# Row-shaped weight products with 512 moving columns, vectors in blocks of 512 and split row transfers in a one-token decoder block

## The chip, the cores and the metric

The kernel runs on one core of one Trainium2 chip. The metric is the device time of one execution in microseconds (us). The kernel before took 415.2, 415.21 and 415.24 us in three runs, median 415.21. A profiled execution is a further run, with its own time.

## The reference

One token (a row of 1024 numbers, bfloat16) passes a decoder block: layer norm, attention over a cache of 65,536 positions with 32 query heads and 4 key/value heads, output projection, residual; then layer norm, a gated feed-forward layer of width 3584, residual.

```
def _A_ref(x, k_cache, v_cache, wq, wo):          # 32 heads of 128, 4 kv heads
    q = (x @ wq).reshape(B, Sq, Hq, Dh).transpose(0, 2, 1, 3)
    ...
    scores = jnp.einsum("bhqd,bhkd->bhqk", q, k) * (Dh ** -0.5)
    p = _softmax(scores, axis=-1)
    o = jnp.einsum("bhqk,bhkd->bhqd", p, v)
    return o.transpose(0, 2, 1, 3).reshape(B, Sq, Hq * Dh) @ wo

def _B_ref(x, w_gate, w_up, w_down):
    return (_gelu(x @ w_gate) * (x @ w_up)) @ w_down

h = x + _A_ref(_layernorm(x), A_k_cache, A_v_cache, A_wq, A_wo)
h2 = h + _B_ref(_layernorm(h), B_w_gate, B_w_up, B_w_down)
```

Every weight and every cache entry is used once, so 173 MB have to come from memory for one row of output.

## The kernel before

All large transfers go through one queue, SyncE's (SP in the profile), in the order of the source, into a pool of four chunks of 4 MB (`chpool`, 32 KB per partition): two for `wq`, then 32 for the caches, two for `wo`, two each for gate, up and down. A chunk is asked for as soon as the chunk four places earlier has been used up. The framework under the kernel gives each engine its instructions in an order of its own that keeps to the dependences; it isn't always that of the source.

A vector of 1024 stands in columns: partition p holds the 8 neighbours 8p to 8p+7 (`x_col`, `h_col`, L152 and L335). The helper `layernorm_cols` (L126 and after) normalises such a vector; its last step, L145, writes bfloat16 columns (`xn_bf`, `hn_bf`).

**Narrow products.** The products with `wq` (L160), gate and up (`ffn_in`, L357) and down (L397) are made with the weights as the stationary operand: 128x128 weights are loaded, and one column of the vector moves through them, which gives 128 outputs, one to a partition. In gate and up the 128 weights of a load lie 28 numbers apart (`f:F:FC`), in down 8 numbers apart (`j:D:DC`), in q they are neighbours. All of them add into one small PSUM tile that is set to zero first: 256 such products for q, 224 each for gate, up and down.

**Wide products.** The output projection (L324) does it the other way round: the vector, padded with zeros to 32 columns (`o2z`), is the stationary operand, and 512 neighbouring weights of each partition move. Four such products stand side by side in the array, at `tile_position` (0, 32q), and add into the row 32q of a PSUM bank; two banks (`at_ps`) hold the two halves of the 1024 outputs, four partial sums each. The result is a row, not a column: L328 and L330 copy the banks to `at_r`, and eight f32 products against a column of ones (L333) add the partial sums and turn them into columns.

Between the parts of the attention nothing is touched by the change: K chunks are transposed by VectorE (L211) and multiplied (L215), the scores are reduced (L225, L226), the softmax is taken on ScalarE (L248), and V chunks are multiplied (L264, L278). Gate's result goes through an approximate gelu on VectorE and ScalarE (L364 to L374) while up's products run; L377 multiplies both into `act_bf`. Down's weights come in pieces of 10, 6, 4, 3, 2, 1, 1 and 1 rows per partition, and the last of them in three transfers, for 8, 8 and 112 partitions. L402 adds the residual, L403 stores the 2 KB of output.

Of the kernel before, what the change touches and what calls it, by code (L numbers as in the profile page):

```python
# [17 lines left out]
def kernel(  # L18
# [13 lines left out]
    nc = tc.nc  # L32
# [18 lines left out]
    DCH = 2  # L51
    CW = DCH * CH * Dh
    assert NCH % DCH == 0
    scale = float(Dh) ** -0.5
    eps = 1e-5
    assert Dh == P and rep * NS == SQ and NT % (CH * NH) == 0 and D % P == 0 and F % P == 0

    const = ctx.enter_context(tc.tile_pool(name="const", bufs=1))
    small = ctx.enter_context(tc.tile_pool(name="small", bufs=2))
# [16 lines left out]
    wq_v = A_wq.rearrange("(p c) n -> p c n", p=P)  # L76
    WB = CW // HD
    assert WB >= 1 and DC % WB == 0
    XU = 16
    XV = P // XU  # L80
    x_in = const.tile([XU, XV, DC], BF16, name="x_in")
    nc.scalar.dma_start(out=x_in[:], in_=A_x[0, 0].rearrange("(u v c) -> u v c", u=XU, v=XV))
    wq_tiles = []
    for c0 in range(0, DC, WB):
        w_sb = chunk("wq_sb")
        wv = w_sb[:, 0:WB * HD].rearrange("p (c n) -> p c n", c=WB)
        nc.sync.dma_start(out=wv, in_=wq_v[:, c0:c0 + WB, :])  # L87
        wq_tiles.extend(wv[:, i, :] for i in range(WB))


    ones_f = const.tile([P, P], F32, name="ones_f")
# [55 lines left out]

    x_ps = misc([P, DC], F32, "x_ps")
    for v in range(XV):
        nc.tensor.matmul(x_ps[:], lhsT=xsel[:, v, :], rhs=x_in[:, v, :], start=(v == 0), stop=(v == XV - 1))  # L150
    x_col = const.tile([P, DC], F32, name="x_col")
    nc.vector.tensor_copy(out=x_col[:], in_=x_ps[:])  # L152
    xn_bf = const.tile([P, DC], BF16, name="xn_bf")
    layernorm_cols(x_col[:], xn_bf[:], "ln1")

    q_ps = misc([P, Hq], F32, "q_ps")
    nc.vector.memset(q_ps[:], 0.0)
    for c in range(DC):
        for h in range(Hq):
            nc.tensor.matmul(q_ps[:, h:h + 1], lhsT=wq_tiles[c][:, h * P:(h + 1) * P], rhs=xn_bf[:, c:c + 1],  # L160
                             start=False, stop=False, skip_group_check=True)
    qT_bf = const.tile([P, Hq], BF16, name="qT_bf")
    nc.vector.tensor_copy(out=qT_bf[:], in_=q_ps[:])
    qsel_ps = misc([P, 4, Hq], F32, "qsel_ps")
# [149 lines left out]
    NW = D // 512  # L314
    at_ps = [misc([P, 512], F32, "at_ps") for _ in range(NW)]
    for w0 in range(0, Hq, WN):
        w_sb = chunk("wo_sb")
        wv = w_sb[:, 0:WN * D].rearrange("p (c n) -> p c n", c=WN)
        nc.sync.dma_start(out=wv, in_=wo_v[:, w0:w0 + WN, :])
        for cc in range(WN):  # L320
            c = w0 + cc
            q = c % 4
            for s in range(NW):
                nc.tensor.matmul(at_ps[s][32 * q:32 * q + 32, :], lhsT=o2z[:, c, :],  # L324
                                 rhs=wv[:, cc, s * 512:(s + 1) * 512],
                                 start=(c < 4), stop=(c >= Hq - 4), tile_position=(0, 32 * q))
    at_r = ktpool.tile([P, D], F32, name="at_r", tag="kt")
    nc.vector.tensor_copy(out=at_r[:, 0:512], in_=at_ps[0][:])  # L328
    for s in range(1, NW):
        nc.scalar.copy(out=at_r[:, s * 512:(s + 1) * 512], in_=at_ps[s][:])  # L330
    hc_ps = misc([P, DC], F32, "hc_ps")
    for j in range(DC):
        nc.tensor.matmul(hc_ps[:, j:j + 1], lhsT=at_r[:, j:D:DC], rhs=ones_f[:, 0:1], start=True, stop=True)  # L333
    h_col = const.tile([P, DC], F32, name="h_col")
    nc.vector.tensor_tensor(out=h_col[:], in0=hc_ps[:], in1=x_col[:], op=ALU.add)  # L335


    hn_bf = const.tile([P, DC], BF16, name="hn_bf")
    layernorm_cols(h_col[:], hn_bf[:], "ln2")
    GB = max(1, CW // F)  # L340
    assert DC % GB == 0

    def ffn_in(wmat, name, pieces):
        ps = misc([P, FC], F32, name)
        nc.vector.memset(ps[:], 0.0)
        wv_all = wmat.rearrange("(p c) n -> p c n", p=P)
        assert sum(pieces) == DC
        for c0 in range(0, DC, GB):
            w_sb = chunk("wgu_sb")
            wv = w_sb[:, 0:GB * F].rearrange("p (c n) -> p c n", c=GB)  # L350
            r0 = 0
            while r0 < GB:
                sz = pieces.pop(0)
                nc.sync.dma_start(out=wv[:, r0:r0 + sz, :], in_=wv_all[:, c0 + r0:c0 + r0 + sz, :])
                for cc in range(r0, r0 + sz):
                    for f in range(FC):
                        nc.tensor.matmul(ps[:, f:f + 1], lhsT=wv[:, cc, f:F:FC], rhs=hn_bf[:, c0 + cc:c0 + cc + 1],  # L357
                                         start=False, stop=False, skip_group_check=True)
                r0 += sz
        return ps  # L360

    g_ps = ffn_in(B_w_gate, "g_ps", [4, 4])
# [9 lines left out]
    nc.vector.tensor_scalar(out=hg[:], in0=g_sb[:], scalar1=0.5, scalar2=None, op0=ALU.mult)  # L372
    gl = small.tile([P, FC], F32, name="gl", tag="gl")
    nc.vector.scalar_tensor_tensor(out=gl[:], in0=th[:], scalar=1.0, in1=hg[:], op0=ALU.add, op1=ALU.mult)  # L374
    u_ps = ffn_in(B_w_up, "u_ps", [4, 2, 1, 1])
    act_bf = const.tile([P, FC], BF16, name="act_bf")
    nc.vector.tensor_tensor(out=act_bf[:], in0=u_ps[:], in1=gl[:], op=ALU.mult)  # L377


    wd_v = B_w_down.rearrange("(p c) n -> p c n", p=P)  # L380
    DN = CW // D
    pieces = [[10, 6], [4, 3, 2, 1, 1, 1]]
    assert sum(map(sum, pieces)) == FC and max(map(sum, pieces)) <= DN
    d_ps = misc([P, DC], F32, "d_ps")
    nc.vector.memset(d_ps[:], 0.0)
    c0 = 0
    for group in pieces:
        w_sb = chunk("wd_sb")
        r0 = 0
        for sz in group:  # L390
            wv = w_sb[:, r0 * D:(r0 + sz) * D].rearrange("p (c n) -> p c n", c=sz)
            last = c0 + sz == FC
            for lo, hi in ((0, 8), (8, 16), (16, P)) if last else ((0, P),):
                nc.sync.dma_start(out=wv[lo:hi], in_=wd_v[lo:hi, c0:c0 + sz, :])
            for cc in range(sz):
                for j in range(DC):
                    nc.tensor.matmul(d_ps[:, j:j + 1], lhsT=wv[:, cc, j:D:DC], rhs=act_bf[:, c0 + cc:c0 + cc + 1],  # L397
                                     start=False, stop=False, skip_group_check=True)
            c0 += sz
            r0 += sz  # L400
    h2 = small.tile([P, DC], BF16, name="h2", tag="h2")
    nc.vector.tensor_tensor(out=h2[:], in0=d_ps[:], in1=h_col[:], op=ALU.add)  # L402
    nc.sync.dma_start(out=out[0, 0].rearrange("(p c) -> p c", p=P), in_=h2[:])  # L403


# [28 lines left out]
```

## Time and profile before

| what | us |
|---|---|
| median of the runs | 415.21 |
| the profiled execution, its own time | 414.91 |
| its span, first to last instruction | 413.1 |
| first narrow product of gate | 368.13 |
| last narrow product of up ends | 396.66 |
| last narrow product of down ends | 410.50 |
| TensorE busy over the span | 256.8 (62%) |
| VectorE busy over the span | 201.9 (49%) |
| memory read over the span | 419 GB/s |

In the groups of instructions, each row is a line of the code, its engine and operation, output and inputs, shapes and count, then busy time, the mean of one in ns, and the engine's idle time ahead of it with what ended it:

```profile
L357 PE MATMUL g_ps<-hn_bf,wgu_sb 128*128 128x1 bf16 x224 | 14.3, 202 | 1.2 <-DVE hn_bf L145 1.2
L160 PE MATMUL q_ps<-xn_bf,wq_sb 128*128 128x1 bf16 x256 | 7.2, 165 | 10.8 <-DMA wq_sb<-in_A_wq_dram 10.8
L397 PE MATMUL d_ps<-act_bf,wd_sb 128*128 128x1 bf16 x224 | 13.6, 198 | 0.3 <-DVE act_bf L377 0.3
```

The mean of one includes what overlaps the next; busy time over the count is the spacing. PE is TensorE's products, PEld its weight loads, DVE VectorE, ACT ScalarE, POOL GpSimd. The PEclk row of the page is the clock that TensorE was granted, as a share of full speed; it is 0.5 in most of the last 80 us.

### The profile page before, as it was taken

The page shows a single profiled execution, that of the slowest core. Times are in us where ns is not written, and L with a number is a line of the kernel's source. Part 1 is how long each engine was busy: PE and PEld are TensorE (multiplying, and loading weights), DVE is VectorE, ACT ScalarE, POOL GpSimd, SP SyncE. Part 2 cuts the span into 40 slices and gives each one's busy share as a digit, 9 for nine tenths or more (in the row PEclk, how much of TensorE's full clock was granted, in tenths as well). Part 3 has the DMA queues.
Part 4 walks back from the last instruction along what each step waited for, and adds up shares of the span by engine and source line. Part 5 has one row for each costly group of instructions (what it writes and reads, how often), then busy time and mean ns, then how long its engine had stood idle before and what let it go on. Part 6 is the DMA issues. An engine that isn't in the chain of part 4 may idle for free.

```text
span 413.1 us, 4925 instructions
## 1 busy us (share of the span) xinstructions
PE 256.8 (62%) x2117; PEld 138.3 (33%) x2117; DVE 201.9 (49%) x254; ACT 35.9 (9%) x135; POOL 27.1 (7%) x100
## 2 busy tenths in 40 slices
PE   1336677698291838765566388191928335479997
PEld 1332222243130314221222233030314113279997
DVE  3107999999393808856474389291910000010000
ACT  1000000070000080000003400000071000000000
POOL 8123000310000210000000000000000000000000
PEclk9999989989886867895959698777796755655555
DMA  8999999999999999999999999999999999999993
GB/s 356 420 439 432 428 435 424 431 431 427 435 428 435 427 432 428 430 431 431 424 435 428 435 428 433 428 435 427 431 431 427 435 428 436 423 431 414 425 409 115
DMA packets 7413, 173.33 MB, mean 420 GB/s; under 512 B 992, under 2 KB 992, under 8 KB 1888
## 3 DMA queue, kind: packets, MB, share of 16 engines
q1 hardware_dynamic: 7360, 173.02, 98.0%
q8 instruction: 16, 0.26, 0.3%
q14 instruction: 5, 0.04, 0.0%
q10 hardware_dynamic: 32, 0.00, 0.0%
HBM read 173.02 MB, written 0.00 MB: 419 GB/s over the span
## 4 chain that ended last, share of the span: by engine, by line
DMA 52%; DVE 23%; PE 15%; issue 9%; SPq 0%; POOLq 0%; ACT 0%; POOL 0%; ACTq 0%
DMA k_sb<-in_A_k_cache_dram 44%; DVE kt L211 19%; DMA v_sb<-in_A_v_cache_dram 8%; PE g_ps L357 3%; PE u_ps L357 3%; PE d_ps L397 3%; PE qk_ps L215 2%; DVE mx L226 2%; DVE sc L225 2%; PE acc_ps L264 1%; PE o_ps L278 0%; SPq L87 0%; POOLq L429 0%; ACT acc_sb L275 0%; PE mxT_ps L233 0%
## 5 line engine op out<-in xcount | busy, mean ns | idle before, releaser
L215 PE MATMUL qk_ps<-kt,qs 128*128 128x512 bf16 x512 | 143.7, 436 | 78.8 <-DVE kt L211 76.7
L211 DVE STREAM_TRANSPOSE kt<-k_sb 128x1024 f32<-128x1024 f32 x128 | 146.2, 1208 | 53.5 <-DMA k_sb<-in_A_k_cache_dram 53.5
L215 PEld LDWEIGHTS <-qs 128*128 128x128 bf16 x512 | 54.9, 107 | 164.5 <-issue 120.9
L248 ACT ACTIVATE pt<-sc,nbias 128x256 bf16<-128x256 f32 x64 | 31.5, 492 | 275.2 <-DVE nbias L241 275.2
L264 PE MATMUL acc_ps<-v_sb,pt 128*32 128x512 bf16 x512 | 38.0, 444 | 13.5 <-DMA v_sb<-in_A_v_cache_dram 13.5
L357 PEld LDWEIGHTS <-wgu_sb 128*128 128x128 bf16 x448 | 28.5, 172 | 1.3 <-issue 1.3
L280 DVE TENSOR_TENSOR oT_all<-o_ps,rl 128x8 bf16<-128x8 f32 x4 | 0.7, 167 | 55.1 <-PE o_ps L278 55.1
L264 PEld LDWEIGHTS <-pt 128*32 128x32 bf16 x512 | 13.9, 107 | 33.0 <-issue 25.2
L225 DVE STREAM_TRANSPOSE sc<-qk_ps 128x512 f32<-128x512 f32 x32 | 22.1, 692 | 2.1 <-PE qk_ps L215 2.1
L226 DVE TENSOR_REDUCE mx<-sc 128x8 f32<-128x512 f32 x32 | 22.0, 688 | 1.1
L278 PE MATMUL o_ps<-sel,acc_sb 128*128 128x8 f32 x32 | 7.5, 364 | 21.8 <-ACT acc_sb L275 21.8
L357 PE MATMUL g_ps<-hn_bf,wgu_sb 128*128 128x1 bf16 x224 | 14.3, 202 | 1.2 <-DVE hn_bf L145 1.2
L278 PEld LDWEIGHTS o_ps<-sel,acc_sb 128*128 128x128 f32 x32 | 7.1, 328 | 23.0 <-ACT acc_sb L275 23.0
L357 PE MATMUL u_ps<-hn_bf,wgu_sb 128*128 128x1 bf16 x224 | 14.3, 202 | 0.0
L173 POOL MEMSET qs<- 128x2048 bf16 x4 | 7.2, 1803 | 102.6 <-PE qk_ps L215 102.6
L160 PE MATMUL q_ps<-xn_bf,wq_sb 128*128 128x1 bf16 x256 | 7.2, 165 | 10.8 <-DMA wq_sb<-in_A_wq_dram 10.8
L397 PE MATMUL d_ps<-act_bf,wd_sb 128*128 128x1 bf16 x224 | 13.6, 198 | 0.3 <-DVE act_bf L377 0.3
L397 PEld LDWEIGHTS <-wd_sb 128*128 128x128 bf16 x224 | 13.6, 164 | 0.2 <-issue 0.2
L177 POOL COPY qs<-qsel 32x32 bf16<-32x32 bf16 x64 | 11.2, 247 | 17.1 <-DVE qsel L168 16.4
L324 PE MATMUL at_ps<-wo_sb,o2z 128*32 128x512 bf16 x64 | 6.9, 609 | 8.5 <-DMA wo_sb<-in_A_wo_dram 8.5
L248 ACT ACTIVATION_READ_ACCUMULATOR pt<-sc,nbias 128x1 f32 x64 | 11.9, 186 | 0.0
L312 POOL MEMSET o2z<- 128x1024 bf16 x1 | 0.9, 950 | 156.6 <-PE acc_ps L264 156.6
(80 smaller groups left out, 61.3 us busy)
## 6 DMA issues: line engine op xcount, KB each, us to landing
k_sb<-in_A_k_cache_dram SPq DMA_DIRECT2D x16, 4096.0 KB, 29.8
v_sb<-in_A_v_cache_dram SPq DMA_DIRECT2D x16, 4096.0 KB, 33.1
wq_sb<-in_A_wq_dram SPq DMA_DIRECT2D x2, 4096.0 KB, 12.1
wo_sb<-in_A_wo_dram SPq DMA_DIRECT2D x2, 4096.0 KB, 36.5
wgu_sb<-in_B_w_gate_dram SPq DMA_DIRECT2D x2, 3584.0 KB, 33.4
wgu_sb<-in_B_w_up_dram SPq DMA_DIRECT2D x1, 3584.0 KB, 31.6
wd_sb<-in_B_w_down_dram SPq DMA_DIRECT2D x1, 2560.0 KB
wgu_sb<-in_B_w_up_dram SPq DMA_DIRECT2D x1, 1792.0 KB, 26.4
```

The source lines that it names most:

```text
L160: nc.tensor.matmul(q_ps[:, h:h + 1], lhsT=wq_tiles[c][:, h * P:(h + 1) * P], rhs=xn_bf[:, c:c + 1], start=False, stop=False, skip_group_ch ...
L173: nc.gpsimd.memset(qs[:], 0.0)
L177: nc.gpsimd.tensor_copy(out=qs[rows, :, s, SQ * i + s:SQ * (i + 1):NS], in_=qsel[rows, :, g * rep:(g + 1) * rep])
L211: nc.vector.transpose(out=kt[:], in_=k32[:, s * W:(s + 1) * W])
L215: nc.tensor.matmul(qk[:], lhsT=st["qs"][:, jt, s, :], rhs=mv[:, :, J, :, t], start=(s == 0 and jt == 0), stop=(s == NS - 1 and jt == 3))
L225: nc.vector.transpose(out=sc.rearrange("p n h s -> p (n h s)"), in_=qk[:])
L226: nc.vector.tensor_reduce(out=st["mx"][:, :, ci], in_=sc.rearrange("p n h s -> p h n s"), axis=AX.XY, op=ALU.max)
L248: nc.scalar.activation(out=pt[:].rearrange("p c n h s -> p (c n) h s")[:, :, r, :], in_=sc[:].rearrange("p c n h s -> p (c n) h s")[:, :, ...
L264: nc.tensor.matmul(acc[32 * c:32 * c + 32, :], lhsT=pt[:, ci % CPH, n, :, :].rearrange("p h s -> p (h s)"), rhs=v_sb[:, n:CH:NN, :], start ...
L278: nc.tensor.matmul(o_ps[:], lhsT=acc_sb[:, t * Dh:(t + 1) * Dh], rhs=sel[:, t:SQ:NS], start=(t == 0), stop=(t == NS - 1))
L357: nc.tensor.matmul(ps[:, f:f + 1], lhsT=wv[:, cc, f:F:FC], rhs=hn_bf[:, c0 + cc:c0 + cc + 1], start=False, stop=False, skip_group_check=True)
L397: nc.tensor.matmul(d_ps[:, j:j + 1], lhsT=wv[:, cc, j:D:DC], rhs=act_bf[:, c0 + cc:c0 + cc + 1], start=False, stop=False, skip_group_check ...
```

## The change

The change does six things.

1. Vectors stand in blocks of 512: partition p holds the 4 neighbours 4p to 4p+3 of each block (D = 2 blocks, F = 7). The views of all weights, of x and of the output follow; a narrow product's 128 weights now lie 4 numbers apart.
2. q, gate, the first six of up's eight rows per partition and down's first six blocks of seven become wide products. Layer norm writes column 0 of a zeroed tile (`xz`, `actz`) that serves as the stationary operand. In `wide_rows` seven (or eight) blocks of a row go to the four places of two banks.
3. A wide result is copied from its banks (`evacuate`) and turned into columns by f32 products against selection columns: `to_columns` with `sel4` for q, gate and up, eight products each; `fold_columns` with `sel2` for the output projection and down, which use one bank with two partial sums, four products each.
4. Up's last two rows and down's last block stay narrow products. They add into the same PSUM tile as the columns of the wide part.
5. `load_rows` splits a transfer: all rows but the last for 128 partitions, then the last row in three transfers, of n, 16 - n and 112 partitions. It is used for both chunks of `wo` (n = 2, 4) and of gate (6, 3), the first of up (1), and down's first two blocks (5, 7).
6. Down's pieces are blocks of 4 rows; the last block comes as 2, 1 and 1 rows, each for all 128 partitions, and the transfers for 8 and 8 partitions are gone.

```diff
+    def load_rows(dst, src, splits):
+        nr = dst.shape[1]
+        if not splits:
+            nc.sync.dma_start(out=dst, in_=src)
+            return
+        if nr > 1:
+            nc.sync.dma_start(out=dst[:, 0:nr - 1, :], in_=src[:, 0:nr - 1, :])
+        lo = 0
+        for n in list(splits) + [P - sum(splits)]:
+            nc.sync.dma_start(out=dst[lo:lo + n, nr - 1:nr, :], in_=src[lo:lo + n, nr - 1:nr, :])
+            lo += n
...
+    xz = const.tile([P, DC, 32], BF16, name="xz")
+    nc.gpsimd.memset(xz[:], 0.0)
+    layernorm_cols(x_col[:], xz[:, :, 0], "ln1")
+    def wide_rows(banks, rows_z, ci, w_row, first, last):
+        for t in range(w_row.shape[-1] // NB):
+            q = t % 4
+            nc.tensor.matmul(banks[t // 4][32 * q:32 * q + 32, :], lhsT=rows_z[:, ci, :],
+                             rhs=w_row[:, t * NB:(t + 1) * NB], start=first, stop=last, tile_position=(0, 32 * q))
...
+    def evacuate(banks, nt, name):
+        r = ktpool.tile([P, len(banks), NB], F32, name=name, tag="kt")
...
+            if b == 0:
+                nc.vector.tensor_copy(out=r[0:kp, b, :], in_=ps[0:kp, :])
+            else:
+                nc.scalar.copy(out=r[0:kp, b, :], in_=ps[0:kp, :])
...
+    def to_columns(dst, r, nt):
+        for b in range(r.shape[1]):
+            nq = min(4, nt - 4 * b)
+            for c in range(C4):
+                nc.tensor.matmul(dst[:, 16 * b + c:16 * b + 4 * nq:C4], lhsT=r[0:32 * nq, b, c:NB:C4],
+                                 rhs=sel4[0:32 * nq, 0:nq], start=False, stop=False, skip_group_check=True)
...
-    for c in range(DC):
-        for h in range(Hq):
-            nc.tensor.matmul(q_ps[:, h:h + 1], lhsT=wq_tiles[c][:, h * P:(h + 1) * P], rhs=xn_bf[:, c:c + 1],
-                             start=False, stop=False, skip_group_check=True)
+    for b in range(2):
+        for hh in range(4):
+            nc.tensor.matmul(q_ps[:, 16 * b + hh:16 * b + 16:4], lhsT=q_r[:, b, hh * P:(hh + 1) * P], rhs=sel4[:],
+                             start=True, stop=True)
...
+    def fold_columns(dst, ps, name):
+        r = ktpool.tile([P, NB], F32, name=name, tag="kt")
+        nc.vector.tensor_copy(out=r[:, 0:NB // 2], in_=ps[:, 0:NB // 2])
+        nc.scalar.copy(out=r[:, NB // 2:NB], in_=ps[:, NB // 2:NB])
+        for c in range(C4):
+            nc.tensor.matmul(dst[:, c:DC:C4], lhsT=r[:, c:NB:C4], rhs=sel2[:], start=False, stop=False,
+                             skip_group_check=True)
...
                 for cc in range(r0, r0 + sz):
-                    for f in range(FC):
-                        nc.tensor.matmul(ps[:, f:f + 1], lhsT=wv[:, cc, f:F:FC], rhs=hn_bf[:, c0 + cc:c0 + cc + 1],
-                                         start=False, stop=False, skip_group_check=True)
+                    ci = t * C4 + cc
+                    if ci < n_wide:
+                        wide_rows(banks, hz, ci, wv[:, cc, :], ci == 0, ci == n_wide - 1)
+                        if ci == n_wide - 1:
+                            to_columns(ps, evacuate(banks, FT, name + "_r"), FT)
+                    else:
+                        for f in range(FC):
+                            k, c = divmod(f, C4)
+                            nc.tensor.matmul(ps[:, f:f + 1], lhsT=wv[:, cc, k * NB + c:(k + 1) * NB:C4], rhs=hz[:, ci, 0:1],
+                                             start=False, stop=False, skip_group_check=True)
...
-    u_ps = ffn_in(B_w_up, "u_ps", [4, 2, 1, 1])
+    u_ps = ffn_in(B_w_up, "u_ps", [(4, (1, 15)), (2, ()), (1, ()), (1, ())], DC - 2)
...
+    wd_splits = [(5, 11), (7, 9)] + [()] * (FT - 2)
+    for t in range(FT):
...
+        if t < FT - 1:
+            load_rows(wv, wd_v[t], wd_splits[t])
+            for cc in range(C4):
+                for s in range(DS):
+                    q = 2 * (cc % 2) + s
+                    nc.tensor.matmul(dw_ps[32 * q:32 * q + 32, :], lhsT=actz[:, t * C4 + cc, :],
+                                     rhs=wv[:, cc, s * NB:(s + 1) * NB], start=(t == 0 and cc < 2),
+                                     stop=(t == FT - 2 and cc >= C4 - 2), tile_position=(0, 32 * q))
+            if t == FT - 2:
+                fold_columns(d_ps, dw_ps, "dw_r")
+            continue
         r0 = 0
-        for sz in group:
...
-            for lo, hi in ((0, 8), (8, 16), (16, P)) if last else ((0, P),):
-                nc.sync.dma_start(out=wv[lo:hi], in_=wd_v[lo:hi, c0:c0 + sz, :])
+        for sz in (2, 1, 1):
+            nc.sync.dma_start(out=wv[:, r0:r0 + sz, :], in_=wd_v[t][:, r0:r0 + sz, :])
```

More of the change, by code (lines that the diff above doesn't have):

```diff
@@ L53 @@
     assert NCH % DCH == 0
+    NB = 512
+    C4 = NB // P
+    DS = D // NB
+    FT = F // NB
     scale = float(Dh) ** -0.5
     eps = 1e-5
-    assert Dh == P and rep * NS == SQ and NT % (CH * NH) == 0 and D % P == 0 and F % P == 0
+    assert Dh == P and rep * NS == SQ and NT % (CH * NH) == 0 and D % NB == 0 and F % NB == 0 and C4 == 4
     const = ctx.enter_context(tc.tile_pool(name="const", bufs=1))
@@ L73, in misc @@
         return ps_m.tile(shape, dtype, name=name, tag="misc")
-    wq_v = A_wq.rearrange("(p c) n -> p c n", p=P)
-    WB = CW // HD
-    assert WB >= 1 and DC % WB == 0
+    def load_rows(dst, src, splits):
[9 more added lines that the diff above has]
+            lo += n
+    wq_v = A_wq.rearrange("(t p c) n -> t p c n", p=P, c=C4)
+    assert C4 * HD == CW
     XU = 16
     XV = P // XU
-    x_in = const.tile([XU, XV, DC], BF16, name="x_in")
-    nc.scalar.dma_start(out=x_in[:], in_=A_x[0, 0].rearrange("(u v c) -> u v c", u=XU, v=XV))
+    x_in = const.tile([XU, DS, XV, C4], BF16, name="x_in")
+    nc.scalar.dma_start(out=x_in[:], in_=A_x[0, 0].rearrange("(t u v c) -> u t v c", t=DS, u=XU, v=XV))
     wq_tiles = []
-    for c0 in range(0, DC, WB):
+    for t in range(DS):
         w_sb = chunk("wq_sb")
-        wv = w_sb[:, 0:WB * HD].rearrange("p (c n) -> p c n", c=WB)
-        nc.sync.dma_start(out=wv, in_=wq_v[:, c0:c0 + WB, :])
-        wq_tiles.extend(wv[:, i, :] for i in range(WB))
+        wv = w_sb[:].rearrange("p (c n) -> p c n", c=C4)
+        nc.sync.dma_start(out=wv, in_=wq_v[t])
+        wq_tiles.append(wv)
     ones_f = const.tile([P, P], F32, name="ones_f")
@@ L118 @@
     nc.vector.tensor_tensor(out=sel[:], in0=sel[:], in1=ident_f[:, 96:128], op=ALU.add)
+    sel4 = const.tile([P, 4], F32, name="sel4")
+    nc.vector.tensor_copy(out=sel4[:], in_=ident_f[:, 0:P:32])
+    sel2 = const.tile([P, 2], F32, name="sel2")
+    nc.vector.tensor_tensor(out=sel2[:], in0=sel4[:, 0:2], in1=sel4[:, 2:4], op=ALU.add)
     OQ = P // Hq
@@ L149 @@
     for v in range(XV):
-        nc.tensor.matmul(x_ps[:], lhsT=xsel[:, v, :], rhs=x_in[:, v, :], start=(v == 0), stop=(v == XV - 1))
+        nc.tensor.matmul(x_ps[:].rearrange("p (t c) -> p t c", t=DS), lhsT=xsel[:, v, :], rhs=x_in[:, :, v, :],
+                         start=(v == 0), stop=(v == XV - 1))
     x_col = const.tile([P, DC], F32, name="x_col")
     nc.vector.tensor_copy(out=x_col[:], in_=x_ps[:])
-    xn_bf = const.tile([P, DC], BF16, name="xn_bf")
-    layernorm_cols(x_col[:], xn_bf[:], "ln1")
@@ L156 @@
-    q_ps = misc([P, Hq], F32, "q_ps")
-    nc.vector.memset(q_ps[:], 0.0)
-    for c in range(DC):
-        for h in range(Hq):
-            nc.tensor.matmul(q_ps[:, h:h + 1], lhsT=wq_tiles[c][:, h * P:(h + 1) * P], rhs=xn_bf[:, c:c + 1],
-                             start=False, stop=False, skip_group_check=True)
+    xz = const.tile([P, DC, 32], BF16, name="xz")
[6 more added lines that the diff above has]
+                             rhs=w_row[:, t * NB:(t + 1) * NB], start=first, stop=last, tile_position=(0, 32 * q))
@@ new lines, in bank_pair @@
+    def bank_pair(name, n=2):
+        return [ps_qk.tile([P, NB], F32, name=name, tag="qk") for _ in range(n)]
+    def evacuate(banks, nt, name):
+        r = ktpool.tile([P, len(banks), NB], F32, name=name, tag="kt")
+        for b, ps in enumerate(banks):
+            kp = 32 * min(4, nt - 4 * b)
+            if b == 0:
+                nc.vector.tensor_copy(out=r[0:kp, b, :], in_=ps[0:kp, :])
+            else:
+                nc.scalar.copy(out=r[0:kp, b, :], in_=ps[0:kp, :])
+        return r
@@ new lines, in to_columns @@
+    def to_columns(dst, r, nt):
[4 more added lines that the diff above has]
+                                 rhs=sel4[0:32 * nq, 0:nq], start=False, stop=False, skip_group_check=True)
+    q_banks = bank_pair("qw_ps")
+    for t in range(DS):
+        for cc in range(C4):
+            ci = t * C4 + cc
+            wide_rows(q_banks, xz, ci, wq_tiles[t][:, cc, :], ci == 0, ci == DC - 1)
@@ L162 @@
+    q_r = evacuate(q_banks, HD // NB, "q_r")
+    q_ps = misc([P, Hq], F32, "q_ps")
+    for b in range(2):
+        for hh in range(4):
+            nc.tensor.matmul(q_ps[:, 16 * b + hh:16 * b + 16:4], lhsT=q_r[:, b, hh * P:(hh + 1) * P], rhs=sel4[:],
+                             start=True, stop=True)
     qT_bf = const.tile([P, Hq], BF16, name="qT_bf")
@@ L313 @@
     nc.gpsimd.tensor_copy(out=o2z[:, :, 0], in_=o2_bf[:])
-    NW = D // 512
-    at_ps = [misc([P, 512], F32, "at_ps") for _ in range(NW)]
+    at_ps = bank_pair("at_ps", 1)[0]
+    wo_splits = [(2, 14), (4, 12)]
     for w0 in range(0, Hq, WN):
@@ L318 @@
         wv = w_sb[:, 0:WN * D].rearrange("p (c n) -> p c n", c=WN)
-        nc.sync.dma_start(out=wv, in_=wo_v[:, w0:w0 + WN, :])
+        load_rows(wv, wo_v[:, w0:w0 + WN, :], wo_splits.pop(0))
         for cc in range(WN):
             c = w0 + cc
[L322 to L330, printed above, removed]
+            for s in range(DS):
+                q = 2 * (c % 2) + s
+                nc.tensor.matmul(at_ps[32 * q:32 * q + 32, :], lhsT=o2z[:, c, :], rhs=wv[:, cc, s * NB:(s + 1) * NB],
+                                 start=(c < 2), stop=(c >= Hq - 2), tile_position=(0, 32 * q))
@@ L331 @@
+    def fold_columns(dst, ps, name):
[5 more added lines that the diff above has]
+                             skip_group_check=True)
     hc_ps = misc([P, DC], F32, "hc_ps")
-    for j in range(DC):
-        nc.tensor.matmul(hc_ps[:, j:j + 1], lhsT=at_r[:, j:D:DC], rhs=ones_f[:, 0:1], start=True, stop=True)
+    nc.vector.memset(hc_ps[:], 0.0)
@@ L334, with ffn_in @@
+    fold_columns(hc_ps, at_ps, "at_r")
     h_col = const.tile([P, DC], F32, name="h_col")
     nc.vector.tensor_tensor(out=h_col[:], in0=hc_ps[:], in1=x_col[:], op=ALU.add)
[L338 to L343, printed above, removed]
+    hz = xz
+    layernorm_cols(h_col[:], hz[:, :, 0], "ln2")
+    assert C4 * F <= CW
+    def ffn_in(wmat, name, pieces, n_wide):
         ps = misc([P, FC], F32, name)
@@ L345, in ffn_in @@
         nc.vector.memset(ps[:], 0.0)
-        wv_all = wmat.rearrange("(p c) n -> p c n", p=P)
-        assert sum(pieces) == DC
-        for c0 in range(0, DC, GB):
+        banks = bank_pair(name + "_w")
+        wv_all = wmat.rearrange("(t p c) n -> t p c n", p=P, c=C4)
+        for t in range(DS):
             w_sb = chunk("wgu_sb")
-            wv = w_sb[:, 0:GB * F].rearrange("p (c n) -> p c n", c=GB)
+            wv = w_sb[:, 0:C4 * F].rearrange("p (c n) -> p c n", c=C4)
             r0 = 0
-            while r0 < GB:
-                sz = pieces.pop(0)
-                nc.sync.dma_start(out=wv[:, r0:r0 + sz, :], in_=wv_all[:, c0 + r0:c0 + r0 + sz, :])
+            while r0 < C4:
+                sz, splits = pieces.pop(0)
+                load_rows(wv[:, r0:r0 + sz, :], wv_all[t][:, r0:r0 + sz, :], splits)
@@ L355, in ffn_in @@
                 for cc in range(r0, r0 + sz):
-                    for f in range(FC):
-                        nc.tensor.matmul(ps[:, f:f + 1], lhsT=wv[:, cc, f:F:FC], rhs=hn_bf[:, c0 + cc:c0 + cc + 1],
-                                         start=False, stop=False, skip_group_check=True)
+                    ci = t * C4 + cc
+                    if ci < n_wide:
[7 more added lines that the diff above has]
+                                             start=False, stop=False, skip_group_check=True)
@@ L359, in ffn_in @@
                 r0 += sz
         return ps
-    g_ps = ffn_in(B_w_gate, "g_ps", [4, 4])
+    g_ps = ffn_in(B_w_gate, "g_ps", [(4, (6, 10)), (4, (3, 13))], DC)
     g_sb = small.tile([P, FC], F32, name="g_sb", tag="g_sb")
@@ L374 @@
     nc.vector.scalar_tensor_tensor(out=gl[:], in0=th[:], scalar=1.0, in1=hg[:], op0=ALU.add, op1=ALU.mult)
-    u_ps = ffn_in(B_w_up, "u_ps", [4, 2, 1, 1])
[L376 to L383, printed above, removed]
+    actz = ptpool.tile([P, FC, 32], BF16, name="actz", tag="pt")
@@ L384 @@
+    nc.gpsimd.memset(actz[:], 0.0)
+    u_ps = ffn_in(B_w_up, "u_ps", [(4, (1, 15)), (2, ()), (1, ()), (1, ())], DC - 2)
+    nc.vector.tensor_tensor(out=actz[:, :, 0], in0=u_ps[:], in1=gl[:], op=ALU.mult)
+    wd_v = B_w_down.rearrange("(t p c) n -> t p c n", p=P, c=C4)
+    DN = CW // (C4 * D)
     d_ps = misc([P, DC], F32, "d_ps")
     nc.vector.memset(d_ps[:], 0.0)
-    c0 = 0
-    for group in pieces:
-        w_sb = chunk("wd_sb")
-        r0 = 0
-        for sz in group:
-            wv = w_sb[:, r0 * D:(r0 + sz) * D].rearrange("p (c n) -> p c n", c=sz)
-            last = c0 + sz == FC
-            for lo, hi in ((0, 8), (8, 16), (16, P)) if last else ((0, P),):
-                nc.sync.dma_start(out=wv[lo:hi], in_=wd_v[lo:hi, c0:c0 + sz, :])
-            for cc in range(sz):
+    dw_ps = bank_pair("dw_ps", 1)[0]
@@ new lines @@
+    wd_splits = [(5, 11), (7, 9)] + [()] * (FT - 2)
+    for t in range(FT):
+        if t % DN == 0:
+            w_sb = chunk("wd_sb")
+        o = (t % DN) * C4 * D
+        wv = w_sb[:, o:o + C4 * D].rearrange("p (c n) -> p c n", c=C4)
+        if t < FT - 1:
+            load_rows(wv, wd_v[t], wd_splits[t])
+            for cc in range(C4):
+                for s in range(DS):
+                    q = 2 * (cc % 2) + s
[5 more added lines that the diff above has]
+            continue
+        r0 = 0
+        for sz in (2, 1, 1):
+            nc.sync.dma_start(out=wv[:, r0:r0 + sz, :], in_=wd_v[t][:, r0:r0 + sz, :])
+            for cc in range(r0, r0 + sz):
@@ L396 @@
                 for j in range(DC):
-                    nc.tensor.matmul(d_ps[:, j:j + 1], lhsT=wv[:, cc, j:D:DC], rhs=act_bf[:, c0 + cc:c0 + cc + 1],
-                                     start=False, stop=False, skip_group_check=True)
-            c0 += sz
+                    k, c = divmod(j, C4)
+                    nc.tensor.matmul(d_ps[:, j:j + 1], lhsT=wv[:, cc, k * NB + c:(k + 1) * NB:C4],
+                                     rhs=actz[:, t * C4 + cc, 0:1], start=False, stop=False, skip_group_check=True)
@@ L402 @@
     nc.vector.tensor_tensor(out=h2[:], in0=d_ps[:], in1=h_col[:], op=ALU.add)
-    nc.sync.dma_start(out=out[0, 0].rearrange("(p c) -> p c", p=P), in_=h2[:])
+    nc.sync.dma_start(out=out[0, 0].rearrange("(t p c) -> p t c", p=P, c=C4), in_=h2[:].rearrange("p (t c) -> p t c", c=C4))
 _INS = ['A_x', 'A_k_cache', 'A_v_cache', 'A_wq', 'A_wo', 'B_x', 'B_w_gate', 'B_w_up', 'B_w_down']
```

## The prediction

> **What bounds the kernel now.** First the chain of waits that ended last; its end, where columns are start, duration, what:
>
> ```profile
> 303.20 33.44 DMA v_sb<-in_A_v_cache_dram
> ...
> 368.13 14.33 PE g_ps L357 x224
> 382.46 14.20 PE u_ps L357 x224
> 396.66 0.02 issue
> 396.68 0.20 DVE act_bf L377
> 396.88 0.04 issue
> 396.92 13.58 PE d_ps L397 x224
> 410.50 0.02 issue
> 410.53 0.17 DVE h L402
> ```
>
> From 368.13 on TensorE never waits: 672 one-column products at 64, 64 and 61 ns set the end (410.50); 2.6 us (h2, output transfer) close the span of 413.1. Then the table by windows, for when the weights had landed (last three columns: granted clock, DMA share, GB/s):
>
> ```profile
> 402.00:404.00 2.00, 2.00 (x37) 2.00 (x37) 0.00 (x0) 0.00 (x0) 0.00 (x0) 0.50 1.03 394
> 404.00:405.00 1.00, 1.00 (x20) 1.00 (x19) 0.00 (x0) 0.00 (x0) 0.00 (x0) 0.50 0.81 213
> 405.00:406.00 1.00, 1.00 (x20) 1.00 (x20) 0.00 (x0) 0.00 (x0) 0.00 (x0) 0.50 0.58 205
> 406.00:407.00 1.00, 1.00 (x20) 1.00 (x20) 0.00 (x0) 0.00 (x0) 0.00 (x0) 0.50 0.57 195
> 407.00:408.00 1.00, 1.00 (x20) 1.00 (x19) 0.00 (x0) 0.00 (x0) 0.00 (x0) 0.50 0.31 113
> ```
>
> The stream ran at some 430 GB/s since the start and ends at 408.0, only 2.5 us before TensorE. So the change can win 2.5 us at most, unless the stream ends earlier too. And it ends unevenly: from 404 on half the rate is left, so half of the 16 DMA engines are done 3 to 4 us before the others. The page's queue list says why:
>
> ```profile
> q8 instruction: 16, 0.26, 0.3%
> ```
>
> In the trace's packet records these 16 packets of 16 KB begin at 19.6, 29.3, 63.0, ... 350.1, ... 406.0 us, and after each the completions of one DMA engine come 1.54 us later than before. The ninth makes one late a second time that the first had hit: eight engines share them. Their number follows TensorE's products (2117 in all, one fetch per some 126). The engines that carried the two 8-partition transfers of the old ending are the early ones: one goes from 403.34 to 404.14, which is 2 x (81 + 15) + 7 x 81 + 15 ns (81 ns per 2 KB row, 15 per completion); a late one takes 407.08 to 407.67, the last seven rows alone.
>
> **The change, part by part.** *Wide products.* The nearest row is the output projection, whose 32-column products of 512 moving columns run four at a time:
>
> ```profile
> 356.13 3.33 PE L324 MATMUL at_ps<-wo_sb,o2z 128*32 128x512 bf16 x32 [6.12 <-DMA wo_sb<-in_A_wo_dram]
> 359.51 0.69 DVE L328 COPY at_r<-at_ps 128x512 f32<-128x512 f32 x1 [15.27 <-PE at_ps L324]
> 359.55 0.58 ACT L330 COPY at_r<-at_ps 128x512 f32<-128x512 f32 x1 [18.58 <-PE at_ps L324]
> 360.35 3.93 PE L333 MATMUL hc_ps<-ones_f,at_r 128*128 128x1 f32 x16 [0.90 <-DVE at_r L328]
> 364.32 0.17 DVE L335 TENSOR_TENSOR h_col<-hc_ps,x_col 128x8 f32<-128x8 f32 x1 [4.12 <-PE hc_ps L333]
> ```
>
> Four take 0.427 us at the granted clock of 0.5 that all this stage has. Gate: 7 blocks per row over 4 places, two rounds, 0.85 us a row, 6.8 for 8 rows against 14.3. Each move into columns costs a copy (0.69) and 8 f32 products of two passes at 0.238 us: 3.8 us. Output projection: its fold needs 4 f32 products, not 8 (1.9 us for 3.9), and half-size copies (0.43 by 0.16 + 256/512 x 0.53): h_col at 361.9 instead of 364.5, gate at 365.5 instead of 368.1.
>
> From there TensorE waits for weights. Gate's second half lands at about 373 (as before), gate ends at 375, its columns at 379.5; up's first half lands at 381, its next two rows at 385.7, so 6 wide rows end at 388, copy and columns at 392.6, two rows of 28 narrow products (64 ns) at 396.2; actz at 396.5. Down's first three blocks have landed by 398, TensorE has caught up at 399. Everything so far is covered by the stream: it could slip 3 us before it cost anything, as block 5 lands at about 405.
>
> *q* (64 wide, a copy, 16 f32 passes) makes q some 4 us later, the first score product 1.2 us later (35.0 to 36.2). VectorE's transposes have six buffers and don't wait; the fifth K transfer was issued at 42.9, 17 us before the stream reached it. Cost nothing; without that cover 1.2 us.
>
> *The stream.* Bytes stay. Split rows and shorter pieces: about 25 more packets of 5.5 ns each in down, about 40 elsewhere, some 20 more completions of 15 ns: +0.8 us per DMA engine. Products recorded fall by 582 (q 256 to 80, gate 224 to 72, up to 114, down to 88, fold 16 to 8) to 1535, so fetches fall from 16 to 11 before the end. Eight engines still get one, three a second; the three end as the late ones do now, at 407.7 + 0.8. The partial transfers shift rows between DMA engines: n partitions on n engines counted from the same end (estimate, from the 8-partition case), so the engine relieved most loses two 2 KB rows in wo, three 7 KB rows (272 ns each) in gate and up, two 2 KB rows in down, with completions 1.2 us; the next 1.0 and 0.9; the eighth none. If the three late ones are those, the stream ends at 408.5 - 1.0 = 407.5; bounds 407.3 and 408.5.
>
> *The new end.* Block 6 is 2.6 us of stream (1.28 + 0.66 + 0.66 as rows before), so block 5 lands at 404.9. Then: landing to first product 0.49 (355.64 to 356.13), two rounds with the last's latency 1.06, copy start 0.05, half copies 0.43, to TensorE 0.12, the fold's 8 passes 1.90, then 32 narrow products. Their weights have a step of 8 bytes, which no row has: bounds 28 ns (L160, step 2 bytes: 3.57/128) and 61 ns (L397, step 16 bytes, the nearest, taken): 1.94 or 0.90, and 0.15 of latency. 404.9 + 4.05 + 1.94 + 0.15 = 411.04, against 410.50. The output in runs of 8 bytes, twice as many: +0.08. Sum +0.62 on the span: 413.1 to 413.7, the profiled 414.91 to 415.5, the median 415.21 to 415.8.
>
> [...]
>
> **The rivals.** *Cheap step.* Two weights in 16 bytes load as fast as neighbours: 32 x 33 ns = 1.05 us less, 414.8. For it: L357 (step 56) costs hardly more than L397 (step 16), so the price doesn't grow with distance; against it: no row between.
>
> *The late engines catch up.* If fewer fetches, or the shift, leave no engine twice late, the stream ends with the engines hit once (1.3 us less by the completions of the last V transfer, 2.3 against 3.6 us behind the first), relieved by 0.6: 406.6, and with the cheap step TensorE ends at 409.1: 413.9. Against: the count above still gives 11.
>
> *Slower: the relief misses.* The engines relieved most aren't the three hit twice. Then the stream ends at 408.5 and each step of the new ending is 1.0 later: 416.8. It decides once the relief of the latest is under 0.7 us. For it: the shift is a straight ramp, the lateness stands in two steps.
>
> *Eight in flight.* SyncE waits for old transfers:
>
> ```profile
> SPq L394 <- DMA wd_sb<-in_B_w_down_dram: 9.3, 2, 5.9
> SPq L394 <- DMA wgu_sb<-in_B_w_up_dram: 5.9, 3, 2.2
> ```
>
> Down's sixth issue (385.96) came as up's second transfer had landed, the seventh (388.14) as its third had: the k-th waits for the (k-8)-th. With 38 transfers where 18 were, block 2 goes out when block 0 has landed (392.5), with 3.4 us of stream still queued. The early engines run dry for 1.4 us, the latest doesn't: nothing. Were it dry too, 417.2.
>
> [...]
>
> **How the numbers follow.** Forecast 415.8: 0.31; cheap step 414.8: 0.22; late engines catch up 413.9: 0.21; relief misses 416.8: 0.22; dry queue 417.2: 0.04. Within 0.2% means 414.4 to 416.0, about what a measurement can tell: forecast (0.26 of it) and cheap step (0.17) make 0.43. Faster 0.26 (the third case and 0.05 of the cheap step), slower 0.31. The range 413.5 to 417.2 leaves some 0.1 at each end; the forecast's own is 415.0 to 416.4.
>
> **What would show it.** Right: q8 at 11 or 12 packets; TensorE waiting for weights from 369 on; last weights at 407 to 408.5; after block 5 some 1.9 us of fold at its line and 32 narrow products at 61 ns. Wrong: narrow products near 30 ns; products of block 6 put ahead of the fold (it would save up to 0.45 us by the sums above); weights landing before 406.6 or holes in the DMA share before 400; up's columns later than 400.

## The result, and the profile after

The changed kernel takes 435.87 us (median of four runs, 435.06 to 436.27) against 415.23 for the kernel before: a ratio of 1.0494, 95% interval 1.0476 to 1.0512. It is 20.6 us slower, where 0.6 was forecast. The profiled execution took 435.97 us, with a span of 434.0.

The end of the chain of waits of the changed kernel, to be held against the chain before (start, duration, what; SPq is SyncE issuing a transfer):

```profile
358.98 26.42 DMA wgu_sb<-in_B_w_gate_dram
385.47 25.53 DMA wd_sb<-in_B_w_down_dram
411.01 0.35 SPq L85
...
412.36 11.98 DMA wd_sb<-in_B_w_down_dram
424.38 1.07 PE dw_ps L467 x8
425.46 0.43 DVE dw_r L389
425.92 0.38 ACT dw_r L390
426.35 2.03 PE d_ps L392 x8
428.38 1.07 PE d_ps L479 x32
```

TensorE's 42 us of products at the end of the old chain are gone; in their place stand transfers. The last five lines are the new ending, part by part as the prediction laid it out, but for the two half copies, which run one after the other. What it waited for came late. The table by windows shows the weights on their way (last three columns: granted clock, DMA share, GB/s):

```profile
360.00:370.00 10.00, 6.53 (x46) 4.01 (x41) 2.09 (x12) 0.37 (x1) 0.55 (x1) 0.50 1.04 264
370.00:380.00 10.00, 1.91 (x16) 0.31 (x8) 0.00 (x0) 0.00 (x0) 0.00 (x0) 0.50 1.00 287
380.00:390.00 10.00, 6.83 (x41) 4.07 (x41) 0.69 (x1) 0.58 (x1) 0.00 (x0) 0.50 1.02 304
390.00:400.00 10.00, 4.34 (x32) 2.02 (x33) 0.96 (x6) 0.23 (x1) 0.00 (x0) 0.50 0.98 259
```

Two of the same windows in the kernel before:

```profile
370.00:380.00 10.00, 10.00 (x161) 10.00 (x161) 0.00 (x0) 0.00 (x0) 0.00 (x0) 0.50 0.98 416
390.00:400.00 10.00, 9.72 (x157) 9.78 (x157) 0.19 (x1) 0.00 (x0) 0.00 (x0) 0.50 0.98 409
```

The reader is to see the last two columns together: the 16 DMA engines are as busy as ever (share 1.0), and move 259 to 304 GB/s where the kernel before moved 409 to 428 in the same ten-microsecond windows from 360 to 400. They aren't short of work; each packet takes longer. In the trace's packet records a 7 KB packet takes 432 ns (median, a tenth over 639) where it took 275 in the kernel before, a 21 KB packet 945 where the same packets take 804 in a kernel below that cuts its rows by columns. After 416, when the split rows are through, 8 KB packets take 309 ns and the stream is back at 409 GB/s.

### The profile page after: what moved, and what is told of

Its sections match the earlier page's. It is cut to its first block, busy times and chain, and to the rows that moved or that the text cites. A ratio compares the mean times of both kernels' runs of the same rounds, so it can differ in the third digit from the quotient of the medians.

```text
span 434.0 us, 3800 instructions
## 1 busy us (share of the span) xinstructions
PE 251.1 (58%) x1535; PEld 111.3 (26%) x1535; DVE 204.2 (47%) x260; ACT 37.8 (9%) x139; POOL 28.3 (7%) x102
## 3 DMA queue, kind: packets, MB, share of 16 engines
q1 hardware_dynamic: 8736, 173.02, 97.6%
## 4 chain that ended last, share of the span: by engine, by line
DMA 65%; DVE 16%; PE 12%; issue 3%; ACT 2%; SPq 1%; ACTq 0%
DMA k_sb<-in_A_k_cache_dram 33%; DVE kt L270 13%; DMA wo_sb<-in_A_wo_dram 9%; PE qk_ps L274 9%; DMA wd_sb<-in_B_w_down_dram 9%; DMA v_sb<-in_A_v_cache_dram 8%; DMA wgu_sb<-in_B_w_gate_dram 6%; ACT pt L307 2%; DVE mx L285 1%; DVE sc L284 1%; PE acc_ps L323 1%; PE d_ps L392 0%; PE o_ps L337 0%; SPq L85 0%; PE d_ps L479 0%
## 5 line engine op out<-in xcount | busy, mean ns | idle before, releaser
L274 PE MATMUL qk_ps<-kt,qs 128*128 128x512 bf16 x512 | 147.8, 449 | 70.4 <-DVE kt L270 69.0
L274 PEld LDWEIGHTS <-qs 128*128 128x128 bf16 x512 | 56.0, 110 | 159.1 <-issue 114.2
L323 PE MATMUL acc_ps<-v_sb,pt 128*32 128x512 bf16 x512 | 37.0, 435 | 15.6 <-DMA v_sb<-in_A_v_cache_dram 15.6
L186 PEld LDWEIGHTS <-xz 128*32 128x32 bf16 x162 | 6.6, 132 | 41.1 <-issue 36.9
L186 PE MATMUL g_ps_w<-wgu_sb,xz 128*32 128x512 bf16 x56 | 7.6, 625 | 12.0 <-DMA wgu_sb<-in_B_w_gate_dram 10.9
L236 POOL COPY qs<-qsel 32x32 bf16<-32x32 bf16 x64 | 11.2, 248 | 19.3 <-DVE qsel L227 18.6
L186 PE MATMUL qw_ps<-wq_sb,xz 128*32 128x512 bf16 x64 | 7.2, 630 | 9.0 <-DMA wq_sb<-in_A_wq_dram 9.0
L467 PE MATMUL dw_ps<-wd_sb,actz 128*32 128x512 bf16 x48 | 6.5, 617 | 7.7 <-DMA wd_sb<-in_B_w_down_dram 7.3
L186 PE MATMUL u_ps_w<-wgu_sb,xz 128*32 128x512 bf16 x42 | 5.7, 625 | 8.6 <-DMA wgu_sb<-in_B_w_up_dram 8.6
```

Source lines behind the costliest of these rows:

```text
L186: nc.tensor.matmul(banks[t // 4][32 * q:32 * q + 32, :], lhsT=rows_z[:, ci, :], rhs=w_row[:, t * NB:(t + 1) * NB], start=first, stop=last, ...
L236: nc.gpsimd.tensor_copy(out=qs[rows, :, s, SQ * i + s:SQ * (i + 1):NS], in_=qsel[rows, :, g * rep:(g + 1) * rep])
L274: nc.tensor.matmul(qk[:], lhsT=st["qs"][:, jt, s, :], rhs=mv[:, :, J, :, t], start=(s == 0 and jt == 0), stop=(s == NS - 1 and jt == 3))
L323: nc.tensor.matmul(acc[32 * c:32 * c + 32, :], lhsT=pt[:, ci % CPH, n, :, :].rearrange("p h s -> p (h s)"), rhs=v_sb[:, n:CH:NN, :], start ...
L467: nc.tensor.matmul(dw_ps[32 * q:32 * q + 32, :], lhsT=actz[:, t * C4 + cc, :], rhs=wv[:, cc, s * NB:(s + 1) * NB], start=(t == 0 and cc < ...
```

## The experiments

The kernel before was measured again beside each round: 415.13 us beside the first four experiments, 415.32 beside the next four, 415.19 beside the last two. Runs of one kernel lie 0.2 to 1.2 us apart, which bounds what a single run can tell.

**Whole rows.** The first question: is it the split rows, the layout in blocks ('layout'), or the mere number of transfers ('many transfers')?

```diff
-    wo_splits = [(2, 14), (4, 12)]
+    wo_splits = [(), ()]
-    g_ps = ffn_in(B_w_gate, "g_ps", [(4, (6, 10)), (4, (3, 13))], DC)
+    g_ps = ffn_in(B_w_gate, "g_ps", [(4, ()), (4, ())], DC)
-    u_ps = ffn_in(B_w_up, "u_ps", [(4, (1, 15)), (2, ()), (1, ()), (1, ())], DC - 2)
+    u_ps = ffn_in(B_w_up, "u_ps", [(4, ()), (2, ()), (1, ()), (1, ())], DC - 2)
-    wd_splits = [(5, 11), (7, 9)] + [()] * (FT - 2)
+    wd_splits = [()] * FT
```

> The changed kernel with every transfer for all 128 partitions (no split rows, 20 large transfers at the end instead of 38). [...] Theory 'layout': reading the weights in blocks of 512 rows is slow; then it stays at 433 to 437. [...]

Measured: 416.58 us, ratio to before 1.0034 (1.0022 to 1.0046), far below the 433 to 437 of 'layout'. Of the 20.6 us lost, 19.3 go with the split rows; the layout is not slow. (From the output projection on this kernel issues 17 large transfers, not the 20 of the expectation.) The same windows in this kernel:

```profile
370.00:380.00 10.00, 6.50 (x42) 4.35 (x41) 0.69 (x1) 0.58 (x1) 0.00 (x0) 0.80 0.99 423
390.00:400.00 10.00, 6.45 (x87) 4.08 (x87) 0.28 (x1) 0.00 (x0) 0.00 (x0) 0.50 1.01 419
```

**The old kernel with split rows.** The change's `load_rows`, its splits for `wo`, gate and up's first transfer, in the kernel before.

```diff
-        nc.sync.dma_start(out=wv, in_=wo_v[:, w0:w0 + WN, :])
+        load_rows(wv, wo_v[:, w0:w0 + WN, :], wo_splits.pop(0))
-                nc.sync.dma_start(out=wv[:, r0:r0 + sz, :], in_=wv_all[:, c0 + r0:c0 + r0 + sz, :])
+                load_rows(wv[:, r0:r0 + sz, :], wv_all[:, c0 + r0:c0 + r0 + sz, :], splits.pop(0))
```

> The kernel before, its layout and narrow products kept, with the split rows of the change put into wo, gate and the first transfer of up (not into down). [...] Layout: 415 to 417, nothing of it is in this kernel. [...]

Measured: 431.64 us, one run (before: 415.13). Five split rows are slow without anything else of the change.

**16 and 112 partitions.**

```diff
-    wo_splits = [(2, 14), (4, 12)]
+    wo_splits = [(16,), (16,)]
...
-    wd_splits = [(5, 11), (7, 9)] + [()] * (FT - 2)
+    wd_splits = [(16,), (16,)] + [()] * (FT - 2)
```

> The changed kernel with each split row as two transfers, for 16 and 112 partitions, in place of three for n, 16 - n and 112. [...] If only the small uneven transfers (n and 16 - n) were to blame: 415 to 418. Layout: 433 to 437.

Measured: 433.24 us, one run. The uneven small pieces are worth about the 2.6 us that are missing to 435.87. (The range of 'layout' holds this time too, but the first two experiments have ruled the layout out.)

**Columns in place of partitions.** Each split row is cut by columns (a quarter, a quarter, a half), each piece for all 128 partitions. If the mere number of transfers costs the time, this kernel is as slow as the change.

```diff
-        for n in list(splits) + [P - sum(splits)]:
-            nc.sync.dma_start(out=dst[lo:lo + n, nr - 1:nr, :], in_=src[lo:lo + n, nr - 1:nr, :])
-            lo += n
+        W = dst.shape[2]
+        for w in (W // 4, W // 4, W // 2):
+            nc.sync.dma_start(out=dst[:, nr - 1:nr, lo:lo + w], in_=src[:, nr - 1:nr, lo:lo + w])
+            lo += w
```

> [...] Many transfers: 430 to 437. Layout: 433 to 437.

Measured: 418.21 us, one run, far below both ranges. As many transfers as in the change, 10640 packets on SyncE's queue against its 8736, and 17.7 us less. One window, against 287 GB/s in the change:

```profile
370.00:380.00 10.00, 6.84 (x44) 4.96 (x44) 1.30 (x6) 0.58 (x1) 0.00 (x0) 0.63 1.03 424
```

The number of transfers and packets costs about 1.6 us (418.21 - 416.58); the other 17.7 (435.87 - 418.21) go with transfers for fewer than 128 partitions.

**Two halves.** Every split row as 64 and 64 partitions (`(64,)` in all four lists of splits).

> The changed kernel with each split row as two transfers for 64 partitions each: no uneven numbers, both halves on all 16 engines with four rows each. [...] If only the uneven numbers of partitions were slow: 416 to 418.

Measured: 438.87 us, one run: as even as a split can be, and slower than the change, far beyond the 416 to 418 expected if only uneven numbers are slow. 7 KB packets take 416 ns in the median, half as much again as the 274 of whole rows; a tenth of them take over 572, about twice as much. None of the pieces is smaller than 128 KB here.

**One split row.** Whole rows, and only gate's first transfer with a last row of 16 and 112 partitions (the edit against the kernel with whole rows):

```diff
-    g_ps = ffn_in(B_w_gate, "g_ps", [(4, ()), (4, ())], DC)
+    g_ps = ffn_in(B_w_gate, "g_ps", [(4, (16,)), (4, ())], DC)
```

> Whole rows everywhere but in gate's first transfer, whose last row goes as 16 and 112 partitions. [...] If the loss came from running out of transfers in flight: 416 to 417, as only one transfer more is issued.

Measured: 420.42 us, one run, 3.8 more than whole rows. The windows show the hole:

```profile
360.00:365.00 5.00, 3.13 (x12) 2.95 (x12) 1.17 (x8) 0.37 (x1) 0.00 (x0) 0.50 0.97 213
365.00:370.00 5.00, 3.71 (x29) 1.06 (x29) 0.54 (x4) 0.00 (x0) 0.55 (x1) 0.50 1.01 360
370.00:380.00 10.00, 2.91 (x25) 1.21 (x27) 0.00 (x0) 0.00 (x0) 0.00 (x0) 0.50 1.01 433
```

For 5 us the stream runs at half its rate, busy engines and all, then at 360, then at 433. 5 x (430 - 213) + 5 x (430 - 360) KB is 1.4 MB, 3.3 us of stream, most of the 3.8. A row of 0.92 MB, 2.1 us of stream, has slowed down its neighbours too: of the 28 KB packets of the transfers behind it a tenth take over 1408 ns, against 1071 with whole rows.

**Short runs of output.** With whole rows TensorE was done 0.4 us before the old kernel's, and yet the span was longer. Its last instruction stood long after the output's issue, so the old kernel was given the new runs of 8 bytes. Its output then stands in another order than the reference asks for; the run is for the time alone.

```diff
-    nc.sync.dma_start(out=out[0, 0].rearrange("(p c) -> p c", p=P), in_=h2[:])
+    nc.sync.dma_start(out=out[0, 0].rearrange("(t p c) -> p t c", p=P, c=4), in_=h2[:].rearrange("p (t c) -> p t c", c=4))
```

> The kernel before with its 2 KB of output stored in runs of 8 bytes, two per partition, in place of 16 bytes, one per partition (the output stands in another order; nothing else is changed). Theory 'short runs': the last transfer's completion comes about 1.9 us later, as in the kernel with whole rows (4.3 us from its issue to the end, against 2.4): 416.8 to 417.3. Theory 'no matter': 415.1 to 415.4.

Measured: 416.93 us, ratio 1.0041 (1.0026 to 1.0057), so 1.6 us. SyncE's waits (in total, times, longest) tell where; first the kernel before, then this one:

```profile
SPq L429 <- DMA out_dram<-h: 0.9, 1, 0.9
```

```profile
SPq L429 <- DMA out_dram<-h: 2.4, 1, 2.4
```

**A mixed kernel.** Gate and six rows of up wide, down with the old narrow products (16 bytes apart) in blocks of four rows, output, x, q and the output projection as before, whole rows.

```diff
+                    if ci < n_wide:
+                        wide_rows(banks, hz, ci, wv[:, cc, :], ci == 0, ci == n_wide - 1)
+                        if ci == n_wide - 1:
+                            to_columns(ps, evacuate(banks, FT, name + "_r"), FT)
...
+    for t in range(FT):
...
+        for sz in ((4,) if t < FT - 1 else (2, 1, 1)):
+            nc.sync.dma_start(out=wv[:, r0:r0 + sz, :], in_=wd_v[t][:, r0:r0 + sz, :])
```

> The kernel before with gate and six rows of up as wide products (F in blocks of 512, columns by sel4), down as narrow products of its old step (16 bytes) in blocks of four rows, x, q, the output projection and the output as before, whole rows in every transfer. Theory: what the change wins is TensorE's lead over the stream in gate and up; without the fold after down's weights, the split rows and the short output runs the end is the last weights (407) plus half a us of latency and 8 narrow products: the product ends at 408.2 instead of 410.5, 412.5 to 413.5 in all. Rival 'down is bound by its own narrow products': they start at 394 with eight rows landed and take 13.6 us, 408 to 409, the same or up to 1 us later: 413 to 414.3. Rival 'nothing to win': 415.

Measured: 413.88 us, ratio 0.9967 (0.9954 to 0.9979): faster, by 1.4 us, inside the rival's range. Its last 64 narrow products ran without a wait from 405.43 to 409.44, so at the very end the narrow products were the bound.

**The mixed kernel with finer pieces.** The edit against the mixed kernel:

```diff
-        for sz in ((4,) if t < FT - 1 else (2, 1, 1)):
+        for sz in ((4,) if t < FT - 2 else (2, 2) if t < FT - 1 else (2, 1, 1)):
```

> The mixed kernel with the last block but one of down's weights in two transfers of two rows, in place of one of four. In the mixed kernel TensorE got this block at 405.43 and then had 64 narrow products of 62 ns ahead of it without a wait, to 409.44. Theory 'backlog of the last blocks': 16 of them are done before the second half lands, and the end comes 0.6 to 0.9 us earlier, 412.9 to 413.4. Rival 'bound by the last weights': no change, 413.7 to 414.1.

Measured: 413.26 us, ratio 0.9956 (0.9943 to 0.9968), the fastest version here, 1.9 us under the kernel before. TensorE ends at 408.8:

```profile
402.84 5.94 PE L433 MATMUL d_ps<-act_bf,wd_sb 128*128 128x1 bf16 x96 [0.42 <-DMA wd_sb<-in_B_w_down_dram]
408.82 0.17 DVE L437 TENSOR_TENSOR h<-d_ps,h_col 128x8 bf16<-128x8 f32 x1 [15.25 <-PE d_ps L433]
```

**Down narrow, 8 bytes apart.** Whole rows, and all of down as narrow products in the change's layout: no wide block, no fold.

```diff
-            if t == FT - 2:
-                fold_columns(d_ps, dw_ps, "dw_r")
-            continue
         r0 = 0
-        for sz in (2, 1, 1):
+        for sz in ((4,) if t < FT - 1 else (2, 1, 1)):
```

> The changed kernel with whole rows (as in the first experiment), and all of down as narrow products with weights 8 bytes apart, in place of six wide blocks, their copies, the fold and the last narrow block. Theory 'the fold is what stands behind the last weights': products end 0.5 us of latency and 8 x 36 ns after the last weights (407), at 408, against 410.1 with whole rows: 414.2 to 414.9. Rival 'the stream decides': 416.3 to 416.8, as with whole rows.

Measured: 414.05 us, ratio 0.9974 (0.9964 to 0.9984), 0.15 below the range and 2.5 under whole rows. h2 starts at 407.90, against 410.13. The copies and the fold did stand behind the last weights. This kernel still has the 8-byte output; whether the short step and 16-byte runs can be had together wasn't tried.

## Why the prediction was wrong, point by point

**The step that failed** is the stream: "Split rows and shorter pieces: about 25 more packets of 5.5 ns each in down, about 40 elsewhere, some 20 more completions of 15 ns: +0.8 us per DMA engine", and with it the 1.0 us of relief. (The terms, estimates, add up as written to 0.66 us, not 0.8.) I priced a short transfer as packets that go by at their own pace in each engine's queue. The runs show that with transfers for part of the partitions the packets around them slow down too: 19.3 us for seven split rows, 3.8 for one. The relief, if there was any, can't be seen beside that.

The trace of before held a sign. From 403.9 to 405.1 us, as the early engines came to the end of the transfers for 8, 8 and 112 partitions, the 2 KB packets in the packet records take 126 ns (median) against 86 in the microsecond before and 85 in the one after, 4 KB packets 232 against 163 and 178. The prediction's own table has it too: a DMA share of 0.81 for 213 GB/s from 404 to 405, and of 0.58 for 205 a microsecond later. The 81 ns per row fit the late engine, which ran its seven rows from 407.08 on, when the share was down to 0.31. That the slow packets here come from those transfers wasn't tested by itself.

Why it slows down, the runs don't show directly. They show what it goes with: fewer than 128 partitions in a transfer (433.24 us with 16 + 112 and 438.87 with 64 + 64, as well as 435.87 with uneven numbers), not packet size or number (418.21 with 10640 packets, cut by columns). The kernel with two halves has 224 more completions in its packet records than whole rows, 16 for each of its 14 additional transfers, as many as each transfer of 4 MB in the kernel before; I read this as all 16 engines carrying each half. No run tells the reading side of a transfer from its writing side; the cause of the slow packets stays open.

**The rest of the sum, read on whole rows**, where it stands free of that:

```profile
405.03 1.04 PE L467 MATMUL dw_ps<-wd_sb,actz 128*32 128x512 bf16 x8 [1.47 <-DMA wd_sb<-in_B_w_down_dram]
406.12 0.42 DVE L389 COPY dw_r<-dw_ps 128x256 f32<-128x256 f32 x1 [12.49 <-PE dw_ps L467]
406.58 0.37 ACT L390 COPY dw_r<-dw_ps 128x256 f32<-128x256 f32 x1 [18.93 <-DVE dw_r L389]
407.01 2.03 PE L392 MATMUL d_ps<-sel,dw_r 128*128 128x2 f32 x8 [0.93 <-ACT dw_r L390]
408.89 1.20 PE L479 MATMUL d_ps<-actz,wd_sb 128*128 128x1 bf16 x32
...
410.32 0.40 SPq L484 DMA_DIRECT2D out_dram<-h  x1
```

- Block 5's products start at 405.03 (forecast 405.39, with the relief). Two rounds 1.04 (priced 1.06) and the fold 2.03 (priced 1.90).
- The two half copies run one after the other (the last one's releaser is the other copy), 0.83 and not 0.43: a term too small by 0.4.
- The narrow products 8 bytes apart take 1.20 us for 32, and 1.99 for up's 56 (35.5 ns each), not 61. The rival of the cheap step held: nearer to 28 than to 61. The 28 ns come from a granted clock of 1.00 (12.90 to 16.50), all the others from 0.50, which the prediction passed over; what neighbours take at 0.50, no run shows.
- TensorE ends at 410.09 (forecast 411.04). The output's end was forecast +0.08 and is 4.3 us from its issue (410.32 to 414.6) against 2.4 before: +1.9, and 1.6 when measured alone. So it was luck that the 415.8 of the sum came close to whole rows' 416.58: two errors of opposite sign, -0.95 and +1.8, and another kernel than the one forecast.
- Gate, up and q: wide products in pairs of rounds as priced; gate's first product on whole rows at 365.81 (forecast 365.5; the prediction's rows, with the end of the last pass counted as before, give 365.8). q is ready 2.7 us later in the changed kernel (30.32 against 27.63), not 4, and its first score product starts at 35.15, against 35.02, not at 36.2: no cost.
- Fetches: 16 became 12 (forecast 11 before the end, 11 or 12 named as the sign):

```profile
q8 instruction: 12, 0.20, 0.2%
```

**The rival "eight in flight"** was given 417.2 and 0.04. In the changed kernel the stream does run dry:

```profile
408.00:412.00 4.00, 3.63 (x66) 3.34 (x70) 0.28 (x1) 0.00 (x0) 0.00 (x0) 0.50 0.71 207
```

Share 0.71 here, when SyncE could issue block 2 only at 411.0 (forecast 392.5), as the first rows of block 0 had landed. That is 1.2 us of stream (4 x 0.29), a consequence of the slow packets as far as the runs tell: with as many transfers cut by columns all of the excess, this included, is 1.6.

**Small transfers** aren't what made the loss. With two halves no piece is under 128 KB, and that kernel loses the most, 22.3 us over whole rows. The 38 transfers cut by columns, the smallest of 64 KB, cost 1.6. What smaller pieces cost by themselves, no run shows.

**What the change could have won** was stated rightly: 2.5 us at most, and 1.9 of them are there in the mixed kernel with finer pieces, which lets TensorE wait for the weights through gate and up and puts neither a fold nor short runs behind the last of them.

## What to carry to other kernels

Here a transfer that left out partitions was not a smaller transfer: seven rows cut by partitions cost 19.3 us, the same rows cut by columns, with all 128 partitions in each piece, 1.6. So try cuts by columns or rows first while a long stream is under way. Read busy engines against bytes moved: a DMA share of 1.00 at 287 GB/s, where the kernel before moved 416, was slow packets (432 ns against 275 for 7 KB), not lack of work. Where the stream sets the end, count what stands behind the last weights: here a fold (2.03 us), two copies (0.83) and runs of 8 bytes in the output (1.6). Ahead of the last weights TensorE had time to spare with wide products: in whole rows it waited 1.44 to 1.47 us for each of down's last four blocks before the narrow one.

## What the runs showed of the hardware that was not expected

One split row of 0.9 MB among 173 MB cost 3.8 us (420.42 against 416.58). After each of the 16 packets of 16 KB on the instruction queue q8 (16 with 2117 products of TensorE, 12 with 1535) the completions of one DMA engine came 1.54 us later in the kernel before, always of one of the same eight, and from 404 to 408 the stream ran at 213 GB/s and less. Weights 8, 16 and 56 bytes apart took 36, 61 and 64 ns for each load with its product, at a granted clock of 0.50; 2 bytes apart they took 28, at 1.00. Storing 2 KB in runs of 8 bytes rather than 16 made the time 1.6 us longer, with SyncE's wait for that transfer at 2.4 us in place of 0.9. TensorE went through the old kernel's last 672 one-column products, 42 us with one pause of 0.3, at a granted clock of 0.50.
